# Attention, gated block and channel MLP on one core: the first channel weights converted in an earlier round and kept in DRAM

## The chip, the cores and the metric

The kernel runs on one core of one Trainium2 chip. The metric is the device time of one execution, in microseconds; smaller is better. Three executions of the kernel before took 945.94 us (median), from 945.16 to 947.19. The execution that was profiled took 946.54 us; its span, from the first to the last instruction, is 944.7 us.

## What is computed

Three stages follow each other: attention with rotary positions, a gated MLP whose gate mixes tokens, and a mixer with a low-rank token product and a wide channel MLP. There are 4 batches of 576 tokens with 512 channels.

```python
x = attention(rotate(q), rotate(k), v)             # 4 x 576 x 512
h = gelu(x @ w_in); u, v = halves(h)               # 512 channels each
v_s = w_sg @ (layer_norm(v) * g_ln) + b_sg         # over tokens
x = x + (u * v_s) @ w_out
u = x + (V.T @ U.T over tokens)(x)
out = u + relu(u @ w_ch1) @ w_ch2                  # 512 -> 2048 -> 512
```

Inputs are float32, but the weights reach the kernel as 8-byte floats, viewed as pairs of 32-bit words. Before a matmul may use such a block, it is converted to float32 and taken apart into a high part (float32r) and a low part (the rest); each product is then three matmuls (high by high, high by low, low by high).

## The kernel before, in words

The state `X[b]` (channels on the partitions, tokens along the free axis) stays in SBUF for all four batches. After attention, PE's order is the order of the program text (`manual_schedule` with PE alone); the order of DVE, ACT, POOL and SP is set by the scheduler of the framework, each engine then running its list in order. SP issues nearly all DMAs, in order too: a DMA whose wait isn't over holds back those behind it.

The gated block is a loop over `b` in 0, 1, 2 (line 801), called a round here. In round b the kernel finishes batch b and prepares batch n = b + 1:

- `s_step(b, d)`, four times: the token mix; PE writes a PSUM tile `m`, DVE takes it (lines 646 and 647) into `g`, ACT and POOL split `g` into `GH` and `GL`.
- `v_step(n, t)`: the v half; ACT applies gelu into a buffer `gt` (line 557; three buffers of 4 KB per partition), DVE and POOL normalise, ACT and POOL split it into `VH` and `VL` (lines 617 and 530).
- `o_step(b, e)`, four times: the output matmul into a PSUM tile `w`, added into `X[b]` by DVE (line 658).
- `y_step`, `z_step`, `h_step`: PE transposes `X[b]` (line 670, tile `t`), ACT and DVE split the transpose into `YH` (line 672) and `YL` (line 678), PE multiplies by U (tile `z`) and by V (tile `q`), DVE adds into `X[b]` (line 700).
- `u_step(n, k0)`, four times: the u half, with ACT's gelu (line 634) into `ug`.

PSUM holds four tiles, used in turn, so a PSUM tile that DVE or ACT hasn't read yet holds up the fourth tile after it. After the loop, batch 3 is finished in the same way (lines 836 to 858), mixed with the first steps of the channel MLP: `c1` multiplies by w_ch1, `c2` by w_ch2, in four groups of 512 hidden channels and five blocks of tokens (lines 868 to 881).

`staged` (line 98) brings a raw block of 128 rows by 512 numbers (512 KB) by DMA and converts it in five operations: ACT's absolute value (line 73) and four on DVE (lines 74 to 77), into a tile `t64`. `weights` (line 713) calls it for the eight blocks of a group (four of w_ch1, four of w_ch2), then ACT makes the high part (line 719) and POOL the low part (line 530, through `less`). For group 0 the raw blocks land in `gt`, the buffers that the gelu uses, and `t64` has two buffers; the eight parts go into the `setA` tiles, which hold w_in until batch 3's v and u halves are computed. All this is called in round 2 and after it (lines 831 to 834 and 847), around the mix of batch 3.

Of the kernel before, what the change touches and what calls it, by code (L numbers as in the profile page):

```python
# [8 lines left out]
F32 = mybir.dt.float32  # L9
# [45 lines left out]
def tile_kernel(ctx: ExitStack, tc: tile.TileContext, qk, vv, tabs, w_in, g_ln, wsgT, b_sg, w_out, u_r, v_r, w1, w2, out):  # L55
    nc = tc.nc

    def f(ap):
        return ap.bitcast(F32)

    def h2(ap):
        return ap.rearrange("p (a b) -> p a b", a=2)

    def bits(ap):

        return ap.bitcast(U32)

    def from_f64(t, raw):

        lo, hi = raw[:, :, 0], raw[:, :, 1]  # L70
        tu = t.bitcast(U32)
        return (
            lambda: nc.scalar.activation(t, hi.bitcast(F32), AF.Abs),
            lambda: nc.vector.tensor_scalar(t, t, F64_LEAST, F64_MOST, ALU.max, ALU.min),  # L74
            lambda: nc.vector.tensor_scalar(tu, tu, 5, 2, ALU.logical_shift_left, ALU.logical_shift_right),
            lambda: nc.vector.scalar_tensor_tensor(tu, hi, 0xC0000000, tu, ALU.bitwise_and, ALU.bitwise_or),
            lambda: nc.vector.scalar_tensor_tensor(tu, lo, 29, tu, ALU.logical_shift_right, ALU.bitwise_or),
        )
# [3 lines left out]
    w_in, w_out, u_r, v_r, w1, w2 = (bits(a) for a in (w_in, w_out, u_r, v_r, w1, w2))  # L82
    B, NHEAD, _, P, S = qk.shape
# [7 lines left out]
    KT = DM // P  # L91
# [6 lines left out]
    def staged(pool, src, tag="raw64", bufs=2):  # L98

        raw = pool.tile([P, 512, 2], U32, tag=tag, name=tag, bufs=bufs)  # L100
        t = pool.tile([P, 512], F32, tag="t64", name="t64", bufs=1 if tag == "raw64" else 2)
        nc.sync.dma_start(raw.rearrange("p n w -> p (n w)"), src)
        for fn in from_f64(t, raw):
            fn()
        return t
# [14 lines left out]
    dram = ctx.enter_context(tc.tile_pool(name="dram", bufs=1, space=bass.MemoryType.DRAM))  # L120
# [303 lines left out]
    def x_hi(b, k):  # L424
        nc.scalar.activation(XH[:, k], X[b][:, k], AF.Copy)

    def x_lo(b, k):
        nc.gpsimd.tensor_tensor(XL[:, k], X[b][:, k], f(XH[:, k]), ALU.subtract)
# [25 lines left out]
    for t in range(T0, NC * NH + LAG):  # L454
# [13 lines left out]
        lo = lows[:-1] if 0 <= t < NC * NH and t % NC in SPLITS else lows[:]  # L468
# [7 lines left out]
        while n_max < upto or ready:  # L476
            m, c = divmod(n_max, NC) if n_max < upto else (NH, 0)
# [29 lines left out]
    p2 = es2.enter_context(tc.tile_pool(name="p2", bufs=1, reuse_waits="tile"))  # L507
    ps2 = ctx.enter_context(tc.tile_pool(name="ps2", bufs=4, space=PSUM, reuse_waits="tile"))

    def ps_tile(name):  # L510
        return ps2.tile([P, 2, 512], F32, tag="ps", name=name)
# [17 lines left out]
    def less(out, a, b):  # L529
        return nc.gpsimd.tensor_tensor(out, a, b, ALU.subtract)  # L530
# [29 lines left out]
    def mm3(ps, pairs, halves):  # L560
        n = len(pairs)
        for j, (l, r) in enumerate(pairs):
            for a in range(halves):
                rr = r[:, a * HALF:(a + 1) * HALF] if halves == 2 else r
                o = ps[:, a, :HALF] if halves == 2 else ps
                nc.tensor.matmul(o, l, rr, start=(j == 0), stop=(j == n - 1))  # L566

    def x_split(b):
        for k in range(KT):
            x_hi(b, k)  # L570
            x_lo(b, k)
        if b % 2 == 0:
            x_tail(b)
# [3 lines left out]
    def x_tail(b):  # L577

        for a in range(2):
            ts = slice(a * D, (a + 1) * D)  # L580
            x = X[b + a][:, :, TAIL]
            nc.scalar.activation(TH[:, :, ts], x, AF.Copy)
            nc.gpsimd.tensor_tensor(TL[:, :, ts], x, f(TH[:, :, ts]), ALU.subtract)
# [43 lines left out]
    def u_step(b, k0):  # L627
        ps = ps_tile(f"u{b}_{k0}")
        pr = []
        for k in range(KT):  # L630
            wh, wl = WUH[:, k, k0 * P:(k0 + 1) * P], WUL[:, k, k0 * P:(k0 + 1) * P]
            pr += [(wh, XH[:, k]), (wh, XL[:, k]), (wl, XH[:, k])]
        mm3(ps, pr, 2)
        nc.scalar.activation(h2(ug[:, k0]), ps[:, :, :HALF], AF.Gelu_apprx_tanh)

    def s_step(b, d):
        ps = ps_tile(f"m{b}_{d}")
        ds_ = slice(d * P, (d + 1) * P)
        pr = []
        for s in range(NC - 1):  # L640
            pr += [(VH[:, s, ds_], WSH[s]), (VH[:, s, ds_], WSL[s]), (VL[:, s, ds_], WSH[s])]
        tail = VT[:, ds_] if b % 2 else VH[:, NC - 1, ds_]
        pr += [(tail, WSH[NC - 1]), (tail, WSL[NC - 1])]
        mm3(ps, pr, 2)
        g = p2.tile([P, S], F32, tag="g", name="g", bufs=2)
        nc.vector.scalar_tensor_tensor(h2(g), ps[:, :, :HALF], gh[:, d:d + 1], h2(bh), ALU.mult, ALU.add)
        nc.vector.tensor_tensor(g, g, ug[:, d], ALU.mult)
        nc.scalar.activation(GH[:, d], g, AF.Copy)
        less(GL[:, d], g, f(GH[:, d]))
# [14 lines left out]
    def y_step(b, s):  # L664

        pp, nt = TS[s], min(2, NC - s)
        pt = ps_tile(f"t{b}_{s}")
        for j in range(nt):
            for k in range(KT):
                nc.tensor.transpose(pt[:pp, j, k * P:(k + 1) * P], X[b][:, k, (s + j) * P:(s + j) * P + pp], ident)  # L670
        YH = p2.tile([P, 2, DM], F32R, tag="YH", name="YH", bufs=2)
        nc.scalar.activation(YH[:pp, :nt], pt[:pp, :nt], AF.Copy)
        if s == NC - 1:
            nc.vector.tensor_tensor(YH[pp:, 0], pt[:pp, 0], f(YH[:pp, 0]), ALU.subtract)
            YS[b, s] = YH[:, 0],
            return
        YL = p2.tile([P, 2, DM], F32R, tag="YL", name="YL", bufs=2)
        nc.vector.tensor_tensor(YL[:pp, :nt], pt[:pp, :nt], f(YH[:pp, :nt]), ALU.subtract)
        for j in range(nt):
            YS[b, s + j] = YH[:, j], YL[:, j]  # L680

    def z_step(b, s):
        if s == 0:
            ZS[b] = ps_tile(f"z{b}")
        pz = ZS[b]
        u4 = U4[:, s].rearrange("p a r -> p (a r)")
        for j, y in enumerate(YS.pop((b, s))):
            nc.tensor.matmul(pz[:, 0, :], u4, y, start=(s == 0 and j == 0), stop=(s == NC - 1))  # L688
        if s == NC - 1:
            Z = p2.tile([P, 2, DM], F32R, tag="YL", name=f"Z{b}", bufs=2)[:, 0]  # L690
            nc.scalar.activation(Z, pz[:, 0, :], AF.Copy)
            nc.vector.tensor_tensor(Z[64:96], pz[64:96, 0, :], f(Z[64:96]), ALU.subtract)
            ZS[b] = Z
# [9 lines left out]
    FG = 512  # L703
# [6 lines left out]
    UH, UL = [flat(XH, KT * WIDE[0])], [flat(XL, KT * WIDE[0])]  # L710
    W = {}

    def weights(pool, g, tiles):

        W[g] = tiles
        for hi, lo, src in ((tiles[0], tiles[1], w1[:, g * 2 * FG:(g + 1) * 2 * FG]), (tiles[2], tiles[3], w2[g * FG:(g + 1) * FG])):
            for k in range(KT):
                t = staged(pool, src[k * P:(k + 1) * P], *(("gt", 3) if g == 0 else ()))
                nc.scalar.activation(hi[:, k], t, AF.Copy)  # L719
                less(lo[:, k], t, f(hi[:, k]))  # L720
                yield
# [59 lines left out]
    def run(fn, b, *which):  # L781
        for x in which:
            fn(b, x)
# [12 lines left out]
    with ExitStack() as es:  # L796
        for x in LASTS:
            es.enter_context(tc.issue_after(x.ins))
        next(ow)
        x_split(1)  # L800
    for b in range(B - 1):
        n = b + 1
        for d in range(KT):
            if d == 1 and n > 1:
                x_split(n)
            s_step(b, d)
            next(ow, None)
        run(v_step, n, 0, 1)
        if b == 0:
            run(v_step, n, 2, 3)  # L810
        run(o_step, b, *range(KT))
        if b > 0:
            run(v_step, n, 2, 3)
        if n < B - 1:
            run(y_step, b, 0, 2)
            v_step(n, 4)
            us = iter(range(KT))
            if n % 2:
                u_step(n, next(us))
            run(z_step, b, *range(NC - 1))  # L820
            y_step(b, 4)
            u_step(n, next(us))
            z_step(b, 4)
            u_step(n, next(us))
            run(h_step, b, 0, 1)
            u_step(n, next(us))
            run(h_step, b, 2, 3)
            run(u_step, n, *us)
        else:
            v_step(n, 4)  # L830
            w = weights(p2, 0, SETA[2:] + SETA[:2])
            for k0 in range(KT):
                u_step(n, k0)
                next(w)
# [106 lines left out]
```

## Time and profile before

| | |
|---|---|
| median of three executions | 945.94 us (945.16 to 947.19) |
| the profiled execution | 946.54 us, span 944.7 us |
| busy: PE, DVE, POOL, ACT | 923.5, 537.8, 375.5, 347.9 us |
| mean granted clock of TensorE | 0.991 of full speed |
| attention | 0 to 312 us |
| rounds 0, 1, 2 and batch 3 | 312 to 567 us |
| channel MLP | 567 to 942 us |

The profile shows one execution. A line number names the line of the kernel that issued an instruction; `t<-gt` means that the tile `t` is written from the tile `gt`. An engine's idle time stands in brackets with what ended it. The granted clock is 1.00 at 2.4 GHz and 0.50 at 1.2 GHz.

### The profile page before, as it was taken

To read this page: it belongs to the slowest core of one execution; us is meant where nothing else is said; L and a number is where in the kernel's file an instruction comes from. 1 tells how busy PE (TensorE), PEld (TensorE's weight loads), DVE (VectorE), ACT (ScalarE), POOL (GpSimd) and SP (SyncE) were. 2 spreads that over 40 slices of the span, in tenths; PEclk is the share of its full clock that TensorE was granted. 3 is DMA by queue.
4 is the path that set the end of the run, shared out by engine and by line. 5 is a ranking of instruction groups with operands and counts; after the bars stand their busy time and mean duration, and the time that the engine had idled before them with its cause. 6 is when DMAs were issued, how large, how long until landed. Compare 5 with 4: busy or idle time off the path is not lost.

```text
span 944.7 us, 13202 instructions
## 1 busy us (share of the span) xinstructions
PE 923.5 (98%) x5180; PEld 784.0 (83%) x5180; DVE 537.8 (57%) x720; ACT 347.9 (37%) x574; POOL 375.5 (40%) x313
## 2 busy tenths in 40 slices
PE   6899999999999999999999999999999999999998
PEld 3588888888886999999999878888888888888887
DVE  7797888787897585334348748643652542222222
ACT  4376666666666443214224243311310320101000
POOL 7788876876725665322426426210210220000000
PEclk7899999999999999999999999999999999999999
DMA  5579867677661400000003200320320210000112
GB/s 178 127 223 190 211 166 180 188 185 186 168 172 44 153 1 1 1 1 23 1 23 113 67 0 28 107 67 3 110 68 1 67 45 0 1 1 23 45 51 84
DMA packets 57300, 77.93 MB, mean 82 GB/s; under 512 B 29755, under 2 KB 33110, under 8 KB 57238
## 3 DMA queue, kind: packets, MB, share of 16 engines
q1 hardware_dynamic: 56928, 77.01, 29.7%
q8 instruction: 41, 0.67, 0.3%
q14 instruction: 21, 0.17, 0.1%
q10 hardware_dynamic: 310, 0.08, 0.0%
HBM read 55.02 MB, written 4.79 MB: 63 GB/s over the span
## 4 chain that ended last, share of the span: by engine, by line
PE 90%; DVE 7%; issue 2%; POOL 1%; DMA 1%; ACT 0%; SPq 0%; ACTq 0%; POOLq 0%
PE a L566 21%; PE r L566 20%; PE pv L278 14%; PE st L251 8%; PE v L566 5%; PE w L566 5%; PE m L566 5%; PE sm L222 4%; PE u L566 4%; DVE t L74 1%; DVE MX L227 1%; PE t L670 1%; PE z L688 1%; DMA raw<-in_qk 1%; DVE K L211 1%
## 5 line engine op out<-in xcount | busy, mean ns | idle before, releaser
L278 PE MATMUL pv<-pc,VV 128*65 128x288 f32 x512 | 144.7, 405 | 0.8 <-DVE sums L299 0.8
L227 DVE TENSOR_REDUCE MX<-sm 128x1 f32<-128x576 f32 (+1 forms) x160 | 119.3, 752 | 45.1 <-PE sm L222 41.8
L251 PE MATMUL st<-Q,K 65*128 65x288 f32 (+3 forms) x640 | 125.5, 319 | 0.0
L760 DVE SCALAR_TENSOR_TENSOR RL<-r,RH 128x1024 fp32r<-128x1024 f32 (+1 forms) x38 | 42.3, 1112 | 123.0 <-ACT RH L759 122.9
L759 ACT ACTIVATE RH<-r 128x1024 fp32r<-128x1024 f32 (+1 forms) x38 | 35.6, 937 | 203.9 <-PE r L566 203.9
L251 PEld LDWEIGHTS st<-Q,K 65*128 65x128 f32 (+3 forms) x640 | 96.1, 179 | 11.1 <-DVE MX L227 0.4
L775 DVE TENSOR_TENSOR X<-a,X 128x256 f32<-128x256 f32 (+4 forms) x65 | 46.4, 745 | 91.3 <-PE a L566 91.3
L254 ACT ACTIVATE pc<-st 128x576 f32<-128x576 f32 x128 | 82.7, 647 | 38.9 <-PE st L251 36.0
L278 PEld LDWEIGHTS pv<-pc,VV 128*65 128x65 f32 x512 | 68.6, 136 | 29.8 <-DVE sums L299 1.1
L566 PE MATMUL a<-RH,setB 128*128 128x512 f32 (+1 forms) x320 | 93.3, 368 | 0.0
L222 PE MATMUL sm<-K,Q 128*128 128x288 f32 (+1 forms) x320 | 76.9, 325 | 10.8 <-ACT K L198 5.1
L566 PE MATMUL a<-RH,setA 128*128 128x512 f32 (+1 forms) x288 | 83.8, 367 | 0.0
L566 PE MATMUL r<-UH,setA 128*128 128x512 f32 (+1 forms) x256 | 73.1, 364 | 0.2 <-DVE X L700 0.2
L566 PE MATMUL r<-UH,setB 128*128 128x512 f32 (+1 forms) x256 | 73.2, 363 | 0.0
L222 PEld LDWEIGHTS sm<-K,Q 128*128 128x128 f32 (+1 forms) x320 | 52.6, 185 | 18.5 <-ACT K L198 6.9
L566 PEld LDWEIGHTS a<-RH,setB 128*128 128x128 f32 x320 | 58.2, 188 | 10.0
L530 POOL TENSOR_TENSOR setB<-t,setB 128x512 fp32r<-128x512 f32 x16 | 20.7, 1295 | 104.7 <-ACT setB L719 93.6
L566 PEld LDWEIGHTS a<-RH,setA 128*128 128x128 f32 x288 | 52.1, 188 | 9.0
L566 PE MATMUL a<-RL,setB 128*128 128x512 f32 (+1 forms) x160 | 58.9, 368 | 0.0
L169 POOL TENSOR_TENSOR Q<-raw,Q 128x576 fp32r<-128x576 f32 x29 | 43.0, 1482 | 35.2 <-ACT Q L164 35.2
L151 POOL TENSOR_TENSOR raw<-raw,tab 128x576 f32<-128x576 f32 x31 | 54.4, 1754 | 5.6 <-DMA raw<-in_qk 5.6
L566 PEld LDWEIGHTS r<-UH,setA 128*128 128x128 f32 x256 | 46.1, 188 | 8.2 <-issue 0.4
(172 smaller groups left out, 1953.7 us busy)
## 6 DMA issues: line engine op xcount, KB each, us to landing
raw<-in_qk SPq DMA_DIRECT2D x31, 576.0 KB
raw<-in_w SPq DMA_DIRECT2D x24, 512.0 KB
K<-Q SPq DMA_DIRECT2D x29, 288.0 KB
VV<-in_vv SPq DMA_DIRECT2D x16, 320.0 KB
rb<-rr SPq DMA_DIRECT2D x15, 288.0 KB
K<-Q SPq DMA_DIRECT2D x29, 144.0 KB
Q<-Q SPq DMA_DIRECT2D x29, 144.0 KB
raw<-in_w_in SPq DMA_DIRECT2D x8, 512.0 KB
```

The source lines that it names most:

```text
L151: lambda: e.tensor_tensor(raw[:, 1], raw[:, 1], tab[:, 1], ALU.mult),
L169: nc.gpsimd.tensor_tensor(Q2[:, :S], rot, f(Q1), ALU.subtract)
L222: nc.tensor.matmul(ps[:TS[t], n, :HALF], Q1[:, t * P:t * P + TS[t]], K1[:, n * HALF:(n + 1) * HALF], start=True, stop=True)
L227: nc.vector.tensor_reduce(MXs[h % 2][:TS[t], t:t + 1], ps[:TS[t], :, :HALF], AX.XY, ALU.max)
L251: nc.tensor.matmul(ps[:kk, n, :HALF], l[:, c * P:c * P + kk], r[:, ns], start=st, stop=not st)
L254: nc.scalar.activation(h2(pc[:kk]), ps[:kk, :, :HALF], AF.Exp, scale=0.125)
L278: nc.tensor.matmul(o, l, r, start=(c == 0 and j == 0), stop=(c == NC - 1 and j == len(pr) - 1))
L530: return nc.gpsimd.tensor_tensor(out, a, b, ALU.subtract)
L566: nc.tensor.matmul(o, l, rr, start=(j == 0), stop=(j == n - 1))
L759: nc.scalar.activation(RH[:, s], ps[:, :, :WIDE[blk]], AF.Relu)
L760: nc.vector.scalar_tensor_tensor(RL[:, s], ps[:, :, :WIDE[blk]], 0.0, f(RH[:, s]), ALU.max, ALU.subtract)
L775: nc.vector.tensor_tensor(X[b][:, e2, xs], ps[:, :n, us], X[b][:, e2, xs], ALU.add)
```

## The change

The conversion of group 0's blocks is split from their use. A generator `first_weights` stages the blocks in rounds 0 and 1, four in each (one after `y_step(b, 4)`, one after `z_step(b, 4)`, two between the `h_step`s), and writes each float32 result (256 KB) to a tile `EARLY` in DRAM. `weights` for group 0 no longer calls `staged`: it brings each block back from `EARLY` into `t64` and makes the high and low part as before.

```diff
+    EARLY = dram.tile([2 * KT, P, 512], F32, tag="w0", name="w0", bufs=1)
+
+    def halves(g):
+        return w1[:, g * 2 * FG:(g + 1) * 2 * FG], w2[g * FG:(g + 1) * FG]
+
+    def first_weights():
+
+        for c, src in enumerate(halves(0)):
+            for k in range(KT):
+                nc.sync.dma_start(EARLY[c * KT + k], staged(p2, src[k * P:(k + 1) * P], "gt", 3))
+                yield
+
     def weights(pool, g, tiles):
 
         W[g] = tiles
-        for hi, lo, src in ((tiles[0], tiles[1], w1[:, g * 2 * FG:(g + 1) * 2 * FG]), (tiles[2], tiles[3], w2[g * FG:(g + 1) * FG])):
+        for c, src in enumerate(halves(g)):
+            hi, lo = tiles[2 * c:2 * c + 2]
             for k in range(KT):
-                t = staged(pool, src[k * P:(k + 1) * P], *(("gt", 3) if g == 0 else ()))
+                if g == 0:
+                    t = p2.tile([P, 512], F32, tag="t64", name="t64", bufs=2)
+                    nc.sync.dma_start(t, EARLY[c * KT + k])
+                else:
+                    t = staged(pool, src[k * P:(k + 1) * P])
                 nc.scalar.activation(hi[:, k], t, AF.Copy)
                 less(lo[:, k], t, f(hi[:, k]))
                 yield
...
+    fw = first_weights()
     for b in range(B - 1):
...
             run(z_step, b, *range(NC - 1))
             y_step(b, 4)
+            next(fw)
             u_step(n, next(us))
             z_step(b, 4)
+            next(fw)
             u_step(n, next(us))
             run(h_step, b, 0, 1)
+            next(fw)
             u_step(n, next(us))
             run(h_step, b, 2, 3)
+            next(fw)
             run(u_step, n, *us)
```

PE's order is the same in both kernels. The other engines' lists move at three places that matter. In the lists, numbers behind a name tell buffers and steps apart. The first four raw blocks are, in order, gt_4020, gt_4059, gt_4102 and gt_4145, their converted tiles t_4021, t_4060, t_4103 and t_4146 (with `t64` for `t` in SP's list).

First place: DVE in round 0, from the add of the first output tile of batch 0 to the split of its transposes. Before:

```order
L658 TENSOR_TENSOR X_66<-w_0_3846,X_66 128x576
L615 TENSOR_SCALAR gt<-gt,bmv,brs 128x512 x2
L658 TENSOR_TENSOR X_66<-w_1_3872,X_66 128x576
L658 TENSOR_TENSOR X_66<-w_2_3898,X_66 128x576
L658 TENSOR_TENSOR X_66<-w_3_3924,X_66 128x576
L678 TENSOR_TENSOR YL<-t_0_3950,YH 128x1024
```

With the change (ahead of these rows stand the first add, the gelu's `L615` and three operations on the first block):

```order
L74 TENSOR_SCALAR t_4060<-t_4060 128x512
L658 TENSOR_TENSOR X_66<-w_1_3873,X_66 128x576
L77 SCALAR_TENSOR_TENSOR t_4021<-gt,t_4021 128x512
L75 TENSOR_SCALAR t_4060<-t_4060 128x512
L76 SCALAR_TENSOR_TENSOR t_4060<-gt,t_4060 128x512
L77 SCALAR_TENSOR_TENSOR t_4060<-gt,t_4060 128x512
L658 TENSOR_TENSOR X_66<-w_2_3899,X_66 128x576
L74 TENSOR_SCALAR t_4103<-t_4103 128x512
L658 TENSOR_TENSOR X_66<-w_3_3925,X_66 128x576
```

The adds stood one behind the other. Now the second stands behind the first operation on the second block, and the fourth behind the first operation on the third block.

Second place: SP from the last DMA of attention's values on. Before:

```order
L326 DMA g_3470<-rr15_3295 64x576 x2
L102 DMA gt_5006<-in_w1 128x1024
L102 DMA gt_5042<-in_w1 128x1024
L102 DMA gt_5078<-in_w1 128x1024
L102 DMA gt_5114<-in_w1 128x1024
```

With the change:

```order
L326 DMA g_3471<-rr15_3295 64x576 x2
L102 DMA gt_4020<-in_w1 128x1024
L102 DMA gt_4059<-in_w1 128x1024
L722 DMA w0_3335<-t64_4021 128x512
L102 DMA gt_4102<-in_w1 128x1024
L102 DMA gt_4145<-in_w1 128x1024
L722 DMA w0_3335<-t64_4060 128x512
```

The load of the third block stands behind the write of the first one to DRAM (`w0` is `EARLY`). In the built program the second load waits for POOL's second `VL` of batch 1's first two token tiles (the buffer `gt` that it takes over), and the write waits for the last operation (line 77) on the first block.

Third place: DVE while the mix of batch 3 runs. Before, from the first mix tile on:

```order
L646 SCALAR_TENSOR_TENSOR g<-m_0_5124,gh,bh 128x576
L647 TENSOR_TENSOR g<-g,ug 128x576
L678 TENSOR_TENSOR YL<-t_0_5158,YH 128x1024
L74 TENSOR_SCALAR t_5365<-t_5365 128x512
L75 TENSOR_SCALAR t_5365<-t_5365 128x512
L74 TENSOR_SCALAR t_5405<-t_5405 128x512
L76 SCALAR_TENSOR_TENSOR t_5365<-gt,t_5365 128x512
L646 SCALAR_TENSOR_TENSOR g<-m_1_5171,gh,bh 128x576
```

With the change:

```order
L646 SCALAR_TENSOR_TENSOR g<-m_0_5173,gh,bh 128x576
L647 TENSOR_TENSOR g<-g,ug 128x576
L678 TENSOR_TENSOR YL<-t_0_5207,YH 128x1024
L646 SCALAR_TENSOR_TENSOR g<-m_1_5220,gh,bh 128x576
L647 TENSOR_TENSOR g<-g,ug 128x576
L678 TENSOR_TENSOR YL<-t_2_5254,YH 128x1024
```

The 32 conversion operations of this part are gone from the list, those ahead of the first row and those between the rows. On ACT, the first four absolute values (line 73) now stand in round 0: the third and fourth ahead of the first `YH` of batch 0.

## Rows read from the trace of the kernel before

**Rows 1.** The page: the span, and busy time of each engine.

```profile
span 944.7 us, 13202 instructions
...
PE 923.5 (98%) x5180; PEld 784.0 (83%) x5180; DVE 537.8 (57%) x720; ACT 347.9 (37%) x574; POOL 375.5 (40%) x313
```

**Rows 2.** PE in time, batch 3's mix: start, length, instruction, [idle before and releaser].

```profile
511.34 0.54 PE L566 MATMUL m<-WS,VH 128*128 128x288 f32 x2 [1.17 <-DVE g L646]
...
521.25 0.50 PE L688 MATMUL z<-YL,U 128*128 128x512 f32 x1 [1.04 <-DVE YL L678]
...
531.84 0.54 PE L566 MATMUL w<-GL,WOH 128*128 128x288 f32 x2 [0.92 <-POOL GL L530]
```

**Rows 3.** DVE in time, the same stretch: a conversion operation, and the delayed `g`.

```profile
493.33 0.42 DVE L74 TENSOR_SCALAR t<-t 128x512 f32<-128x512 f32 x1
...
510.48 0.81 DVE L646 SCALAR_TENSOR_TENSOR g<-m,gh,bh 128x576 f32<-128x576 f32 x1
```

**Rows 4.** The tile gt: conversions in ns (min/median/max), first and last start.

```profile
L73 ACT ACTIVATE t<-gt x8: 655/667/685, 489.2 to 525.8; 128x512 f32<-128x512 f32 x8
L76 DVE SCALAR_TENSOR_TENSOR t<-gt,t x8: 685/691/1676, 493.7 to 531.2; 128x512 uint32<-128x512 uint32 x8
L77 DVE SCALAR_TENSOR_TENSOR t<-gt,t x8: 685/951/1773, 494.6 to 532.4; 128x512 uint32<-128x512 uint32 x8
```

**Rows 5.** DVE in time, round 0: the last three adds, and the two `YL`.

```profile
369.41 1.41 DVE L658 TENSOR_TENSOR X<-w,X 128x576 f32<-128x576 f32 x2
371.50 0.76 DVE L658 TENSOR_TENSOR X<-w,X 128x576 f32<-128x576 f32 x1 [0.68 <-PE w L566]
374.18 2.36 DVE L678 TENSOR_TENSOR YL<-t,YH 128x1024 fp32r<-128x1024 f32 x2 [1.92 <-ACT YH L672]
```

**Rows 6.** ACT in time, round 0.

```profile
369.13 1.16 ACT L617 ACTIVATE VH<-gt 128x512 fp32r<-128x512 f32 x2 [3.32 <-DVE gt L615]
373.12 1.94 ACT L672 ACTIVATE YH<-t 128x1024 fp32r<-128x1024 f32 x2 [2.83 <-PE t L670]
```

**Rows 7.** POOL in time, round 0.

```profile
364.45 2.54 POOL L530 TENSOR_TENSOR VL<-gt,VH 128x512 fp32r<-128x512 f32 x2 [1.38 <-ACT VH L617]
...
369.84 2.52 POOL L530 TENSOR_TENSOR VL<-gt,VH 128x512 fp32r<-128x512 f32 x2 [1.38 <-ACT VH L617]
```

**Rows 8.** The chain that ended last, round 0: start, length, what.

```profile
372.32 1.64 PE t L670 x13
373.95 3.18 PE u L566 x24
377.14 1.86 PE z L688 x8
```

**Rows 9.** SP and ACT in time: two raw loads issued, and ACT waiting for the second.

```profile
442.31 0.33 SPq L102 DMA_DIRECT2D gt<-in_w  x1
...
498.77 0.33 SPq L102 DMA_DIRECT2D gt<-in_w  x1
...
502.81 0.69 ACT L73 ACTIVATE t<-gt 128x512 f32<-128x512 f32 x1 [1.07 <-DMA gt<-in_w]
```

**Rows 10.** Busy us (instructions) of PE, PEld, DVE, ACT, POOL; clock; DMA share, GB/s.

```profile
442.31:446.00 3.69, 3.69 (x30) 3.69 (x29) 1.42 (x2) 0.63 (x1) 0.00 (x0) 1.00 0.47 147
```

**Rows 11.** The same columns, early in attention: PE idle, then at work again.

```profile
25.10:27.70 2.60, 0.00 (x0) 0.00 (x0) 2.57 (x2) 0.00 (x0) 2.60 (x2) 0.99 0.90 256
27.70:29.10 1.40, 0.01 (x1) 0.01 (x1) 1.40 (x3) 0.00 (x0) 0.47 (x2) 0.50 0.27 63
29.10:34.50 5.40, 5.40 (x17) 3.32 (x18) 2.68 (x4) 0.05 (x1) 5.26 (x5) 0.50 0.65 187
34.50:38.00 3.50, 3.36 (x20) 2.40 (x19) 3.06 (x6) 1.34 (x3) 0.43 (x1) 1.00 0.03 5
```

**Rows 12.** The same columns, round 1 from the last split to the mix.

```profile
437.00:453.40 16.40, 16.40 (x125) 16.35 (x124) 5.51 (x9) 7.50 (x12) 6.54 (x7) 1.00 0.11 33
```

**Rows 13.** POOL in time, ahead of batch 3's mix.

```profile
493.43 5.32 POOL L530 TENSOR_TENSOR VL<-gt,VH 128x512 fp32r<-128x512 f32 x2 [1.39 <-ACT VH L617]
```

## The prediction

> **What bounds the kernel now.** I read the page first: PE is busy for 923.5 of 944.7 us [rows 1], so only PE's idle time, or a lower clock, can move the end. After attention I went through PE in time, since a mean over the span hides where it idles. The reader should see three waits of PE in batch 3's mix: 1.17 us for a `g`, 1.04 for a `YL`, 0.92 for a `GL` [rows 2], 3.13 us together. The first ended as DVE finished a `g` begun at 510.48 [rows 3], and DVE was late because eight blocks were being converted there [rows 4]. Then I read DVE, ACT, POOL and the chain in round 0, where the change puts four of the blocks. There PE waits only for DVE's last add, which ends at 371.50 + 0.76 = 372.27 [rows 5], and goes on with the transposes at 372.32 [rows 8]. What stands ahead of that add decides this case.
>
> **What is taken away in batch 3's mix.** Gone there are 8 x 4 DVE operations and 8 of ACT. DVE's cost 0.42 us for the first two kinds [rows 3] and 0.69 to 1.77 for the other two [rows 4]; ACT's cost 0.67 each. None was on PE, so the gain is only what PE waited behind them: all three waits, **-3.1 us**. Bounds are 0 and -3.1. I take the whole, because without the conversions each `g`, `YL` and `GL` follows its matmul directly. The eight reads back from DRAM are new there. The first two are issued in round 1, long before; each later one waits until POOL has finished a low part two blocks earlier. POOL's small operations for batch 3's last gelu now stand behind a low part that waits for such a read. The cover: POOL's two `VL` took 5.32 us in this place [rows 13] and take 2.54 without DVE's conversions beside them [rows 7], so about 2.8 us of waiting costs nothing; if the cover is gone, that is the third rival.
>
> **What is added in round 1.** Four blocks are four times some 2.5 us on DVE (0.42 + 0.42 + 0.69 + 0.95), 10 us. DVE is idle for 16.4 - 5.5 = 10.9 us from the last split to the mix [rows 12], and the block operations stand behind that split, not ahead of the output adds. ACT and POOL are idle for over half of it. I cost this at nothing; what spills over delays the first `g` of a mix whose PSUM tile PE wants three tiles later.
>
> **What is added in round 0.** This is the term that counts. The buffers `gt` are free only as gelus are done, so the four raw loads are late, and the lists put adds behind them. Step by step:
>
> - The second load waits for POOL's second `VL` of batch 1, which ends at 364.45 + 2.54 = 366.99 [rows 7]. A raw load alone, issued at 442.31, had moved 147 GB/s x 3.69 us = 542 KB, all its bytes, by 446.0 [rows 10]: 3.7 us. With another load behind it, ACT could begin 4.04 us after the issue [rows 9]. I take 3.7: landed at 370.7.
> - ACT 0.67, then DVE's first operation on it 0.42: 371.8. Then come the second add (0.70, half of 1.41) [rows 5] and the last operation on the first block: 0.69 to 1.77, median 0.95 [rows 4]. That is 373.4. ACT's second `VH`, done at 370.3 before [rows 6], now stands behind the 0.67, so that POOL's `VL` falls beside this operation, which is why 1.77 can't be excluded.
> - Now SP may issue the write of the first block, 0.33 us as for a load [rows 9], and only then the third load: 373.8. Its duration, with a 256 KB write ahead of it in the queue, shows nowhere. It is bounded by 3.7 (the write costs nothing) and 4.04 + 1.85 = 5.9 (half a load more, for half the bytes). I take the middle, 4.8: 378.6.
> - ACT 0.67, DVE's first operation on the third block 0.42, and then at last the fourth add, 0.76: 380.4.
>
> PE stands at the transposes until 380.4, not 372.3: **+8.1 us**. With the lower ends throughout (3.7, 0.69, 3.7) it is 6.7, with the upper ones (4.04, 1.77, 5.9) 10.5. Nothing hides it, since PE has no other work in its list there.
>
> The Trainium skill (DMA: Bandwidth & Descriptors, section "Anatomy of one DMA") gives a transfer some 2.0 us fixed and the bytes at 436 GB/s, measured on another issuing path; an estimate by that page is 3.2 us for 512 KB. The trace shows 3.7 to 4.0 and decides; by the page's figure the delay would be 6.0.
>
> **The restart.** PE would be idle for about 8 us but for single transposes. In attention it idled from 25.1; after 2.6 us the granted clock fell from 0.99 to 0.50, and stayed there through the first 5.4 us of full work, back at 1.00 after that [rows 11]. Half the clock for 5.4 us costs 2.7 us. At the full clock something smaller shows: the two `YL` now stand behind six operations on the third and fourth block, 380.4 + 3.3 + 2.4 = 386.1, while PE wants the second `YL` some 0.7 us into the `z` matmuls, at 380.4 + 1.64 + 3.18 + 0.7 = 385.9 [rows 5, 8]: 0.2 us. So this term is 0.2 to 2.7; I take **+2.7**, since the only long idle times in the trace end in half the clock, and slow matmuls hide the 0.2.
>
> **The sum.** -3.1 + 8.1 + 2.7 = +7.7 us. Against the profiled execution, 946.54 + 7.7 = 954.2. The median of the runs lies 0.6 lower, so **953.6 us**. The parts outside the span don't change.
>
> **The rivals.**
>
> - *Faster (0.06).* The adds aren't held, because the raw blocks are there when DVE comes to them, and only -3.1 is left: 942.8 us. It decides at the third block: it would have to lie in SBUF by 370.4 for the last add to end at 372.3. By the rows the second block lands only at 370.7, and the third is issued after it. For this speaks only that DVE and the DMA queue have idle time there; against it stand both load rows.
> - *Held, but the full clock stays (0.18).* The single transposes keep the clock up: -3.1 + 8.1 + 0.2 = +5.2, 951.1 us. For it: the idle time isn't unbroken, as it was in the row. Against: PE works for well under a tenth of that time.
> - *Held, and the gain in batch 3 is lost (0.10).* The reads from DRAM come late and POOL's small operations wait behind them, so that PE waits for `VL` where it waited for `g`: +10.8, 956.7 us. Against: POOL's cover of 2.8 us. For: no such read is in the trace. The Trainium skill (the same page and section) says that the completion of a transfer is most of the fixed cost, and heaviest where the target is HBM. No run here shows a large write into DRAM with someone waiting for it; ACT's operation on the third block does wait for the first block's write, since it takes over its tile. By that rule the third block's first operation would be later than the load lets it be, which is another way to the same upper end.
> - *The hold and the gain nearly cancel (0.04).* The delay would have to be under 5 us with the full clock, below my lower end: 944 to 948 us.
>
> **How the numbers follow.** The forecast itself has 0.62. Its own bounds run from 949.7 (6.7 + 0.2 - 3.1 = +3.8) to 956.0 (10.5 + 2.7 - 3.1 = +10.1); with the lost gain the top is 959. The range of 949 to 957.5 holds the forecast, the rival at the full clock and most of the lost gain, and leaves out about 0.15. A measurement of this kernel can tell some 0.2% from no change, 1.9 us. Faster by more than that is the first rival, 0.06; within it is most of the last, 0.03; slower is the rest, 0.91.
>
> **What would show it.** Right: in round 0, an add (line 658) that follows a first operation (line 74) which waited for ACT, which waited for a DMA into `gt`; PE idle for 7 to 10 us at the transposes; a granted clock near 0.5 for some us after them; no wait of PE over 0.5 us in batch 3's mix. Wrong: adds in round 0 that end by 373, a round 1 in which PE waits, or a span that moves while PE's idle time doesn't.

## The result, and the profile after

The changed kernel takes **954.4 us** (median of 6 runs, 952.89 to 955.58), the kernel before 945.75 in the same comparison (944.54 to 947.19). The ratio is 1.0091, 95% interval 1.0078 to 1.0104: slower by 8.6 us. The profiled execution took 955.58 us, its span is 953.8 us (944.7 before).

The page of the changed kernel, span and busy time:

```profile
span 953.8 us, 13247 instructions
...
PE 925.1 (97%) x5179; PEld 785.9 (82%) x5180; DVE 536.9 (56%) x720; ACT 348.0 (36%) x574; POOL 372.2 (39%) x313
```

PE's waits from the end of attention to 600 us, changed kernel (us in total, times, longest):

```profile
PE t L670 <- DVE X L658: 9.2, 3, 4.2
PE w L566 <- POOL GL L530: 0.6, 1, 0.6
PE a L566 <- DVE RL L777: 0.6, 1, 0.6
```

Against [rows 1], PE is busy 1.6 us longer with the same matmuls (the trace lacks the record of one) and idle for the rest of the difference. The three waits of [rows 2], in batch 3's mix, are gone; in their place stands a larger one, in three pieces, at the transposes of round 0. The wait for `GL` listed here is another one, at 361.90, in round 0. (Lines behind 712 have moved: 760 of the kernel before is 777 now, 719 is 736.) The chain that ended last, in round 0 (start, length, what):

```profile
365.30 2.55 POOL VL L530 x2
367.87 4.18 DMA gt<-in_w
372.13 0.67 ACT t L73
372.83 0.43 DVE t L74
...
373.84 1.36 DVE t L77
...
375.66 4.77 DMA gt<-in_w
380.53 0.67 ACT t L73
381.23 0.43 DVE t L74
381.65 0.68 DVE X L658
382.37 3.03 PE t L670 x13
385.40 4.60 PE u L566 x24
390.01 1.86 PE z L688 x8
```

Read it from the top: POOL's `VL` frees a buffer, the second raw block is loaded, ACT and DVE begin on it; then line 77 on the first block, and only then the third load; its first operation on ACT and DVE, and at last the fourth add. The transposes, which started at 372.32 before [rows 8], start at 382.37. Behind them the transposes and the matmuls of `u` take 7.63 us instead of 4.82. SP and then DVE in the same stretch (start, length, instruction, [idle before and what ended it]) show who waited for whom:

```profile
375.23 0.33 SPq L722 DMA_DIRECT2D w<-t  x1
375.66 0.87 SPq L102 DMA_DIRECT2D gt<-in_w  x2
```

```profile
373.84 1.36 DVE L77 SCALAR_TENSOR_TENSOR t<-gt,t 128x512 uint32<-128x512 uint32 x1
...
376.91 0.75 DVE L658 TENSOR_TENSOR X<-w,X 128x576 f32<-128x576 f32 x1
381.23 0.43 DVE L74 TENSOR_SCALAR t<-t 128x512 f32<-128x512 f32 x1 [3.57 <-ACT t L73]
381.57 0.75 DVE L658 TENSOR_TENSOR X<-w,X 128x576 f32<-128x576 f32 x1
```

The third add ends at 377.66. DVE then has nothing to do for 3.57 us, though the last output tile lay in PSUM: the operation ahead of its add waited for a block that was still on its way. The same stretch by windows (busy us and instructions of PE, PEld, DVE, ACT, POOL; clock; DMA share, GB/s):

```profile
368.00:372.40 4.40, 4.40 (x34) 4.14 (x32) 4.19 (x8) 0.90 (x2) 2.23 (x3) 1.00 0.38 123
372.40:375.00 2.60, 0.33 (x2) 0.14 (x1) 2.30 (x4) 0.91 (x2) 1.26 (x1) 0.96 0.00 0
375.00:382.37 7.37, 0.48 (x1) 0.18 (x1) 3.74 (x8) 0.66 (x1) 0.00 (x0) 0.50 0.73 213
382.37:388.20 5.83, 5.83 (x26) 5.83 (x27) 5.66 (x9) 2.73 (x3) 0.00 (x0) 0.50 0.12 45
388.20:394.00 5.80, 5.80 (x40) 5.36 (x39) 0.83 (x2) 1.24 (x2) 0.00 (x0) 0.98 0.12 45
```

PE works for 0.8 of 10 us, the granted clock falls to 0.50 on the way, and it is still 0.50 for the first 5.83 us of full work, as in attention [rows 11].

Where the 9.1 us of the span came from is read from the start of the same matmul in both traces, since PE's order is the same:

| PE's first matmul of | before | after | later by | step |
|---|---|---|---|---|
| `t` (round 0) | 371.31 | 372.13 | 0.82 | |
| `u` behind it | 373.71 | 385.06 | 11.35 | |
| the next `t` | 378.83 | 391.71 | 12.88 | +12.06 in round 0 |
| `m`, batch 3's third | 511.34 | 522.80 | 11.46 | -1.42 |
| `t`, `r` behind it | 522.57 | 532.54 | 9.97 | -1.49 |
| `z`, batch 3's mix | 532.47 | 541.26 | 8.79 | -1.18 |
| `q` | 542.43 | 550.85 | 8.42 | -0.37 |
| `r`, channel MLP | 589.38 | 598.68 | 9.30 | +0.88 |

Between the next `t` and batch 3's mix, through the whole of round 1, nothing moves by more than 0.05 us. The 0.82 at the top is there before any converted block is in the way: POOL's and DVE's work at 322 us is late already, PE meets it in the 0.6 us wait for `GL` at 361.90, and the gelu ahead of `VL` starts at 365.65 instead of 364.80.

### The profile page after: what moved, and what is told of

Same layout as the page of the kernel before. It is cut to its first block, busy times and chain, and to the rows that moved or that the text cites. A ratio compares the mean times of both kernels' runs of the same rounds, so it can differ in the third digit from the quotient of the medians.

```text
span 953.8 us, 13247 instructions
## 1 busy us (share of the span) xinstructions
PE 925.1 (97%) x5179; PEld 785.9 (82%) x5180; DVE 536.9 (56%) x720; ACT 348.0 (36%) x574; POOL 372.2 (39%) x313
## 4 chain that ended last, share of the span: by engine, by line
PE 83%; DVE 8%; DMA 3%; ACT 2%; POOL 2%; issue 2%; SPq 0%; ACTq 0%; DVEq 0%; POOLq 0%
PE a L566 21%; PE r L566 19%; PE pv L278 13%; PE st L251 8%; PE m L566 5%; PE sm L222 4%; PE u L566 4%; PE w L566 4%; PE v L566 3%; DVE t L74 2%; PE t L670 1%; DMA gt<-in_w 1%; PE z L688 1%; DMA Q<-Q 1%; DVE MX L227 1%
## 5 line engine op out<-in xcount | busy, mean ns | idle before, releaser
L566 PE MATMUL a<-RL,setA 128*128 128x512 f32 (+1 forms) x144 | 52.9, 368 | 0.6 <-DVE RL L777 0.6
```

## The experiments

The theory: PE's hold in round 0 (9.2 us) comes from the order of DVE's list, adds behind operations on blocks whose loads are late; 2.8 us more are lost at the lower clock; batch 3's mix gives back some 4.4. Rivals: four blocks' work costs DVE this much anywhere in the round; the slow stretch isn't the clock; the third block adds nothing to the second; the gain isn't the conversions'. Each ratio below is to the kernel before on the same chip (946.25 us for the first four, 945.66 for the last two), five rounds each. Line numbers have moved by a few again in most of them (670, the transposes, is 672 or 673).

| | us | ratio, 95% interval | as us of 945.75 |
|---|---|---|---|
| the change | 954.4 | 1.0091 (1.0078 to 1.0104) | +8.6 |
| order undone in round 0 | 941.91 | 0.9947 (0.9934 to 0.9960) | -5.0 |
| PE kept at work | 952.83 | 1.0065 (1.0053 to 1.0077) | +6.1 |
| third and fourth block moved | 950.09 | 1.0033 (1.0020 to 1.0045) | +3.1 |
| no conversion at all | 942.36 | 0.9953 (0.9940 to 0.9966) | -4.4 |
| w_ch2 early only | 943.02 | 0.9969 (0.9958 to 0.9981) | -2.9 |
| w_ch1 early only, in order | 941.41 | 0.9955 (0.9941 to 0.9968) | -4.3 |

### The order of round 0 undone

`y_step` keeps its last two split instructions in `LY`, and in round 0 the staging is queued behind them.

```diff
-            next(fw)
+            convert(b)
...
+    def convert(b):
+        with ExitStack() as es:
+            if b == 0:
+                for x in LY:
+                    es.enter_context(tc.issue_after(x.ins))
+            next(fw)
```

> The change, but in round 0 the conversions are queued on ACT behind the last YH and on DVE behind the last YL of batch 0, so that no add and no split of the transposes stands behind a raw block. Theory (the hold is a matter of order: PE stood 9.2 us at the transposes because the adds stood behind blocks whose loads were late, and 2.8 us more were lost at the lower clock after it): both go, 954.4 - 12.0 = 942.4 us, 941.5 to 943.5, and the granted clock stays at 1.00 through round 0. Rival (the 10 us of work for four blocks costs DVE about the same wherever in the round it stands): the adds of the low-rank product come late instead and PE waits for PSUM tiles there, 946 to 951 us.

Measured: 941.91 us, 0.9947. PE's longest wait from 320 to 620 us is 0.6. DVE and PE in round 0:

```profile
372.49 0.76 DVE L658 TENSOR_TENSOR X<-w,X 128x576 f32<-128x576 f32 x1 [0.43 <-PE w L566]
375.16 2.35 DVE L680 TENSOR_TENSOR YL<-t,YH 128x1024 fp32r<-128x1024 f32 x2 [1.92 <-ACT YH L674]
...
381.80 0.83 DVE L74 TENSOR_SCALAR t<-t 128x512 f32<-128x512 f32 x2
```

```profile
373.30 1.64 PE L672 MATMUL t<-ident,X 128*128 128x128 f32 x13 [0.52 <-DVE X L658]
```

The same four blocks are converted in the same round; only their place in two lists is another. The windows with the same columns say that their work is there, and that PE doesn't feel it (PE is busy for 15.00 of 15 us in both, DVE for 12.32 instead of 5.14). First this kernel:

```profile
380.00:395.00 15.00, 15.00 (x115) 14.95 (x114) 12.32 (x18) 7.79 (x13) 5.85 (x4) 1.00 0.23 71
```

The same window of the kernel before:

```profile
380.00:395.00 15.00, 15.00 (x114) 14.96 (x113) 5.14 (x8) 5.14 (x9) 5.61 (x4) 1.00 0.01 1
```

The rival that charged the work itself falls. This kernel beats both.

### PE kept at work during the hold

```diff
         pt = ps_tile(f"t{b}_{s}")
+        if b == 0 and s == 0:
+            for i in range(80):
+                nc.tensor.transpose(pt[:, i % 2, :P], ident, ident)
```

> The change, and ahead of batch 0's first transposes PE makes 80 transposes of the identity into the same PSUM tile, some 8 us of work that nothing needs, while it would stand idle. Theory (2.8 us of the loss are the matmuls that ran at half the clock after the wait): the clock stays near 1.00, the adds come no earlier, 954.4 - 2.8 = 951.6 us, 951.0 to 952.4. Rival (the slow stretch after the wait comes from the late splits and DMA traffic, not from the clock): 954.4 us as with the change, or more if the extra work is in the way.

Measured: 952.83 us, 1.0065: by the ratios 2.5 us less than the change. The median lies 0.4 us above the range expected; the kernel before was 0.5 us slower on this chip too, and by the ratio it is 951.9. PE, then the windows (same columns):

```profile
370.32 8.89 PE L670 MATMUL t<-ident 128*128 128x128 f32 x80
379.06 0.49 PE L673 MATMUL t<-ident,X 128*128 128x128 f32 x3
381.46 1.64 PE L673 MATMUL t<-ident,X 128*128 128x128 f32 x13 [1.91 <-DVE X L658]
```

```profile
368.00:379.40 11.40, 11.40 (x102) 11.31 (x100) 7.46 (x11) 1.83 (x3) 2.57 (x2) 1.00 0.43 127
379.40:381.46 2.06, 0.15 (x2) 0.00 (x1) 1.15 (x3) 0.66 (x1) 0.00 (x0) 1.00 0.62 247
381.46:388.40 6.94, 6.94 (x46) 6.08 (x47) 5.90 (x9) 3.28 (x4) 0.00 (x0) 1.00 0.21 78
```

The fourth add comes no earlier: it starts at 380.65, 0.9 us before that of the change, but the end of attention came 1.8 us earlier in this trace, and the second load took 5.12 us until ACT began instead of 4.26 (see the last section). The clock stays at 1.00, and the 13 transposes take 1.64 us again, not 3.03. What is left of the slow stretch is in `z`: its eight matmuls start at 386.12 and the next tile at 388.31, 2.19 us instead of 1.85, because `YL` is late. In these traces the clock was worth 2.8 us of the restart; 0.3 us of late splits show once it is up, and 2.5 us are left as the gain.

### The third and fourth block moved

The same `convert` with `LY`, for the third and fourth call alone; on DVE it waits for batch 0's fourth add, on ACT for the last `YH`.

```diff
-        nc.vector.tensor_tensor(h2(X[b][:, e]), ps[:, :, :HALF], h2(X[b][:, e]), ALU.add)
+        LY[1] = nc.vector.tensor_tensor(h2(X[b][:, e]), ps[:, :, :HALF], h2(X[b][:, e]), ALU.add)
...
```

> The change, but only the third and fourth block of round 0 are moved: on DVE behind batch 0's fourth add, on ACT behind the last YH. Blocks one and two stay where the change has them. Theory (two steps make the hold: the second block's first operation ahead of the second add, and the third block's load, 4.8 us, ahead of the fourth): the third add ends at 377.6 in the changed kernel's trace, the fourth would end at 378.3 instead of 382.3, so 4.0 us less, 950.4 us; if the shorter wait keeps the clock up, 947.6. Rival (the third load holds nothing that the second doesn't hold already): 953.5 to 955 us.

Measured: 950.09 us, 1.0033. The chain and the windows:

```profile
367.17 5.58 DMA gt<-in_w
...
377.69 1.34 DVE X L660 x2
...
379.08 3.04 PE t L672 x13
382.12 3.65 PE u L566 x24
```

```profile
371.40:376.40 5.00, 0.42 (x2) 0.14 (x1) 3.28 (x6) 1.18 (x2) 1.26 (x1) 0.98 0.01 2
376.40:379.08 2.68, 0.48 (x1) 0.18 (x2) 2.59 (x4) 0.00 (x0) 0.00 (x0) 0.50 0.87 193
379.08:383.00 3.92, 3.92 (x18) 3.92 (x19) 1.23 (x1) 1.87 (x2) 0.00 (x0) 0.50 0.74 270
```

The third and fourth add now follow each other, and PE starts 3.3 us earlier than with the change (379.08 for 382.37). Of these, 0.9 come from the end of attention (the first transpose starts at 371.22 here, at 372.13 there); on the other side the second block's load took 5.58 us here instead of 4.18. At equal loads that makes 3.8 us where 4.0 was expected. So both blocks held PE, as the theory has it. The clock fell all the same, for a shorter stretch: 6.69 us for transposes and `u` instead of 4.82, 1.9 us where the change lost 2.8. The first two blocks' place alone still makes this kernel slower than before, by 3.1 us (1.9 to 4.3), although the gain in batch 3's mix is in it.

### No conversion at all

The kernel before, with float32 numbers from another input in place of group 0's blocks:

```diff
-                t = staged(pool, src[k * P:(k + 1) * P], *(("gt", 3) if g == 0 else ()))
+                if g == 0:
+                    t = p2.tile([P, 512], F32, tag="t64", name="t64", bufs=2)
+                    nc.sync.dma_start(t, qk[k, 0, 0, :, :512])
+                else:
+                    t = staged(pool, src[k * P:(k + 1) * P])
```

> The kernel before, but group 0's blocks aren't converted: eight blocks of float32 numbers of the same size are loaded from another input straight into the tile that the conversion would fill, so the first group's channel weights are other numbers and 8 x 5 operations are left out. It measures what the change can win at most. Theory (DVE's conversions made PE wait three times in batch 3's mix; between the two traces the steps there are worth 4.4 us, more than the 3.1 us that the profile puts down as waits): 945.75 - 4.4 = 941.3 us, 940.8 to 942.0. Rival (only the waits as listed are the price, and the rest of the difference is a shift from elsewhere): 942.6 us. Rival (a read that is waited for takes the conversions' place): 944.5 us or more.

Measured: 942.36 us, 0.9953, 4.4 us less than before (3.2 to 5.7). The step table, made for this trace, has the same four falls: -1.41 at `m`, -1.49 at `t` and `r`, -1.17 at `z`, -0.38 at `q`, together 4.45. The bare 3.1 lies just outside the interval. The median as it stands, 942.36, is 0.4 us above the range of the theory and near the rival's 942.6; but the kernel before was 0.5 us slower on this chip, and the ratio (941.3 us) and the step table speak for the theory. The loads in the conversions' place are half as large and need no `gt` buffer, so the 4.4 us are the price of the conversions together with their loads. The kernel with round 0's order undone is as fast within the intervals, so it has everything that taking this work away can bring.

### One half of the blocks at a time

First w_ch2 alone: `first_weights` yields without work for the first four blocks, which `weights` stages as before, so round 0 is untouched.

```diff
             for k in range(KT):
+                if c == 0:
+                    yield
+                    continue
                 nc.sync.dma_start(EARLY[c * KT + k], staged(p2, src[k * P:(k + 1) * P], "gt", 3))
...
-                if g == 0:
+                if g == 0 and c == 0:
+                    t = staged(p2, src[k * P:(k + 1) * P], "gt", 3)
+                elif g == 0:
```

> Only the four w_ch2 blocks are converted early, in round 1, and held in DRAM; the four w_ch1 blocks are staged in round 2 as in the kernel before, and round 0 is as it was before. Theory (the price is paid by what stands among batch 3's mix on DVE; the w_ch1 blocks stood ahead of the first mix tile, where PE doesn't wait, so that the early w_ch2 blocks bring the whole gain, and round 1 hides their work): 945.75 - 4.4 = 941.4 us, 940.8 to 942.3, no wait of PE over 0.5 us between 500 and 545 us. Rival (the gain goes by the number of blocks taken out of this part, whichever they are): half of it, 943.6 us. Rival (round 1 has a hold of its own, which round 0's hid): 945 us or more.

Measured: 943.02 us, 0.9969: no hold, but a third of the gain is missing too. The intervals overlap with those of the whole gain; the step table of this trace says which third: the fall at `m`, 1.42 with the change, is 0.07 here, and the others are there (1.48, 1.18, 0.37). One wait of PE is left in the mix, and the profile shows why, in the waits, on POOL, ACT and DVE:

```profile
PE m L566 <- DVE g L646: 1.1, 1, 1.1
```

```profile
493.68 5.31 POOL L530 TENSOR_TENSOR VL<-gt,VH 128x512 fp32r<-128x512 f32 x2 [1.39 <-ACT VH L617]
```

```profile
500.27 0.67 ACT L73 ACTIVATE t<-gt 128x512 f32<-128x512 f32 x1 [1.23 <-POOL setA L530]
```

```profile
500.97 0.80 DVE L74 TENSOR_SCALAR t<-t 128x512 f32<-128x512 f32 x1 [3.13 <-ACT t L73]
...
509.12 1.66 DVE L77 SCALAR_TENSOR_TENSOR t<-gt,t 128x512 uint32<-128x512 uint32 x1
510.71 0.80 DVE L646 SCALAR_TENSOR_TENSOR g<-m,gh,bh 128x576 f32<-128x576 f32 x1
```

The w_ch1 blocks do stand ahead of the first `g`, but they aren't done in time. POOL's `VL` takes 5.31 us beside them, the third block waits for POOL's low part to free its tile, DVE stands for 3.13 us, and the first `g` starts at 510.71, as late as in the kernel before. The theory's word that PE doesn't wait for these blocks was wrong.

Then w_ch1 alone, in round 0 with the order of the first experiment:

```diff
             for k in range(KT):
+                if c == 1:
+                    yield
+                    continue
                 nc.sync.dma_start(EARLY[c * KT + k], staged(p2, src[k * P:(k + 1) * P], "gt", 3))
...
```

> The other half alone, without the hold: only the w_ch1 blocks are converted early, in round 0, in the order of the first experiment (behind batch 0's last splits); the w_ch2 blocks are staged around batch 3's mix as before. In the built order 11 of their 16 DVE operations now stand ahead of the first mix tile and the last ends ahead of the second YL. Theory (what stands among the mix tiles costs): the later steps go, those at the transposes, z and w, and the first, at the third mix tile, stays: 945.75 - 3.0 = 942.8 us, 942.0 to 944.4. Rival (the w_ch1 blocks have no part in it): 945.2 to 946.5 us. Rival (all of the gain, since half the work is enough to end DVE's lateness): 941.4 us.

Measured: 941.41 us, 0.9955, the whole gain, which the theory had only for its rival. DVE ahead of the mix:

```profile
506.95 1.66 DVE L76 SCALAR_TENSOR_TENSOR t<-gt,t 128x512 uint32<-128x512 uint32 x1
508.53 0.80 DVE L646 SCALAR_TENSOR_TENSOR g<-m,gh,bh 128x576 f32<-128x576 f32 x1
```

With four blocks instead of eight in this part, the w_ch2 blocks move forward into the place of the others, the first `g` starts 2 us earlier than in [rows 3], and no wait of PE over 0.5 us is left in the mix. Both kernels leave four blocks in this part. What differs is how much of their work DVE's list has ahead of the first `g`: all 16 operations with the w_ch1 blocks, as in the kernel before, and 11 of 16 with the w_ch2 blocks. That this number alone decides wasn't tested by itself. Four blocks early were enough when they were the first four, and not when they were the last.

## Why the prediction was right

The median of 954.4 us stands 0.8 above the forecast of 953.6. **The hold** was the term that counts, and it came by the steps forecast: the second load behind POOL's `VL`, line 77 on the first block, the write and the third load on SP, the third block's first operation, the fourth add. From the end of `VL` to PE's start the forecast has 13.4 us (366.99 to 380.4), the trace 14.5 (367.87 to 382.37). The second load took 4.26 us until ACT began, not 3.7; line 77 took 1.36, not 0.95; the third load 4.87 against 4.8. The thirteen transposes start 10.05 us later than before, 9.2 without the 0.82 from the end of attention, where 8.1 was forecast. The size was off by line 77 and by the load, taken from the time in which its bytes had moved [rows 10]: they had moved after 3.70 us here too, but ACT began 0.56 us later. The row with ACT waiting behind a load, 4.04 [rows 9], was nearer. That the third load came so close is luck: 4.8 was the middle of two bounds, and the fourth load, which moved beside it, wasn't in the account. The write ahead of the third load cost at most 1.0 us of the hold: that load also waits for POOL's `VL` of the next two token tiles (in the first experiment SP waits for it alone), which ended at 374.65, and it was issued at 375.66. That the adds' place and not the blocks' work does it is shown by the first experiment, and that the third block holds PE beyond the second by the third one. By the Trainium skill (DMA: Bandwidth & Descriptors, section "Anatomy of one DMA") the estimate was 3.2 us; the traces differ, with 4.18, 4.77 and 5.58 us.

**The restart**, 2.7 forecast, was 2.8 (7.63 less 4.82), and PE kept at work gets 2.5 of it back. The rival at the full clock falls by the window at 0.50, and its 0.2 us for late splits is the 0.3 us seen with PE kept at work.

**The gain** was forecast at -3.1 and was -4.5 in the trace (1.42 + 1.49 + 1.18 + 0.37), and -4.4 in the kernel without the conversions (0.9953). This is the term that was mis-sized, and the prediction's bounds for it, 0 and -3.1, don't hold what was measured: the sum of the listed waits of PE isn't the price of what causes them. At each of the three places the matmuls come 0.25 to 0.45 us earlier than the listed wait accounts for (1.42 for 1.17, 1.49 for 1.04, 1.18 for 0.92), and 0.37 more comes at `q`, where no wait was listed. PE's ends are modelled, so part of a stall can stand as work in the rows; that this is the whole of it was not shown.

**Round 1 at nothing** and **POOL's cover** held: no step in the table between round 0 and the mix, and none of PE's waits names a `VL`. The rival that lost the gain in batch 3 falls. The Trainium skill's rule (the same page and section) that the completion of a transfer is heaviest where the target is HBM was part of that rival. The trace doesn't show it at work on the path: the first block's write had moved its bytes by 376.86, and ACT's operation on the third block began at 380.53, behind its load. A wait for a write does show in other traces here (last section), with another reason.

**Not forecast:** +0.9 at the channel MLP. Far from the change, the scheduler put line 777's `RL` ahead of the last operation of the next group's first block; that block's high part came later on ACT, with the next `RH` behind it, and PE waited 0.6 us for `RL` in a place where it hadn't. The kernel with the extra transposes has that order too, and a step of 0.8 there; the other four that convert early have the old order and no such step. The 0.82 us at the end of attention doesn't look like the change's either: that stretch came between 1.1 us earlier and 1.0 later in the experiments' traces, and 1.0 and 0.1 us earlier in two that convert the same blocks there.

Together: 12.9 - 4.5 + 0.9 = 9.3 at the channel MLP by the traces, 9.1 at the end, and 8.6 by the medians, where the forecast had 7.7. An error of 1.1 on the hold and one of 1.4 on the gain have opposite signs, and two terms that weren't forecast add 1.7. That the median lies within 0.8 of the forecast is luck in part; that it is slower, and by the hold, is not.

**Left open:** whether a fourth `gt` buffer would end the wait for `VL` and for line 77. It wasn't tried.

## What to carry to other kernels

Work moved to a place where an engine is idle isn't free if a scheduler may put it ahead of what another engine waits for: look in the engine's list at what stands in front of each result that the bottleneck wants, and at when its data can land. Here the same conversions cost 12 us ahead of four adds and nothing behind them. To size a gain, take the work out in a throwaway kernel, rather than add up the waits that the profile lists.

## What the runs showed of the hardware

- The same 512 KB load, issued by SP into the same free buffer, took 4.18 us in one kernel and 5.58 in another. Its DMA packets show where the time went: in the second, 126 of its 128 packets had ended by 370.81; a 16 KB packet of the instruction queue (q8) ran from 370.61 to 371.56, and the last two began at 371.55 and 371.97 and ended at 372.33. ACT began at 372.84. In the changed kernel such a packet ran from 371.57, when the load's last one had just ended. In the kernel with the extra transposes it ran from 369.09 to 370.02, and the load's last packet ended at 370.45. That the two share a DMA engine is a reading of these times; the records don't name the engine.
- From the end of a load's last packet to the operation that waited for it, it took 0.56 us in the changed kernel, 0.51 with the third and fourth block moved and 0.73 with the extra transposes. Bytes moved isn't yet data to work on.
- A write can hold its source for long when a load stands ahead of it: with the order undone, the second block's write (256 KB) was issued at 386.02, and ACT's operation on the fourth block, which takes over that tile, began at 391.23 and waited for the write at the end, 5.2 us after the issue. The write's packets began only at 388.59 and ended at 390.63; those of the 512 KB load that SP issued just before it, at 385.55, ran from 386.61 to 389.99. The first block's write, issued at 385.12 with nothing ahead of it, had moved its bytes by 386.75. On ACT and SP:

```profile
391.23 0.67 ACT L73 ACTIVATE t<-gt 128x512 f32<-128x512 f32 x1 [1.37 <-DMA w<-t]
```

```profile
386.02 0.40 SPq L724 DMA_DIRECT2D w<-t  x1
```

- Transposes of 128 columns, one after the other for 8.89 us, kept the granted clock at 1.00 through them and through the 2 us of near idleness that followed, where the change without them had 0.50.
